# Half a block of padding ahead of PE's first turning, and batch 0's third turning in another order

## The chip, the cores and the metric

One core of one Trainium2 chip runs the kernel. The metric is the device time of one execution in microseconds (us). A single profiled execution gives the trace; the engines in it are PE (TensorE: matmuls, with PEld for its weight loads), DVE (VectorE), ACT (ScalarE), POOL (GpSimd) and SP (SyncE, here the queue that issues most DMAs).

## What is computed

Chunked attention over 4 batches, 8 heads, 768 positions, head size 64, followed by a mixer with a rank-32 product over the positions and a two-layer network over 512 channels. Everything is float32.

```
for c in range(nc):                       # chunks of 32, context 16 left, 8 right, 8 memory slots
    k_full = np.concatenate([mem_k, k_ctx], axis=2)
    v_full = np.concatenate([mem_v, v_ctx], axis=2)
    scores = scale * np.matmul(q_c, k_full.transpose(0, 1, 3, 2))
    a = np.exp(scores - max); a = a / (a.sum + 1e-09)
    out[:, :, c_start:c_end] = np.matmul(a, v_full)
x = out.transpose(0, 2, 1, 3).reshape(B, S, H * D)
u = x + (x^T @ U @ V)^T                   # U: 768 x 32, V: 32 x 768
result = u + np.maximum(u @ w_ch1, 0.0) @ w_ch2    # 512 -> 2048 -> 512
```

## The kernel before

Operands of the large products are split into a high and a low part (`uh`/`ul`, `w1h`/`w1l`, `w` as a pair, `hh`/`hl`), and three products of parts replace one. The weights U, V, w_ch1 and w_ch2 arrive as 64-bit words and are decoded on chip by a chain of steps (class `Words`, lines 235 to 281): `begin` on ACT, `shift`, `power`, `mantissa` and `join` on DVE (the join of some on POOL), then a cast to the high part on ACT and a subtraction for the low part (`lower`, line 420).

Batch 0 is a head that runs alone, written out by hand in `attention(0, xs)` (lines 840 to 980). Its 768 positions are taken in three parts, T = 0, 1, 2 ("turnings" of keys, queries and probabilities). For each T: `s_turn(T)` makes the scores (line 735), `s_weights` takes the maximum and the exponential into `pt`, `t_part(T, s)` turns the probabilities on PE (line 789) and copies them to `pT` on ACT (line 792), `av_part(T)` multiplies them with V's rows (64 fp32 matmuls, line 809, 128 records in the trace), `s_sums(T)` gives the row sums and their reciprocals (lines 766 to 771), and av_part then writes two tiles of x on DVE (four instructions, line 821). `collect(t)` (line 833) adds x(t) times the spread U to the rank product; `turn_x` (line 1184) turns x for the first block of the mixer; `spread_v` (line 300) copies V's three decoded column groups from 32-row groups to 96 rows with a matmul each (line 304), cast on ACT (line 309) and subtracted on DVE (line 310).

The words of a unit n of `stream()` are w1 of f=0, w2 of f=0, w1 of f=1, and so on; `advance(n)` moves that generator n steps, so its decoding steps stand in the engines' queues where `advance` is called. `take(n)` issues the next n loads of `LOADS`; `a0` is w1 of f=0, `b0` is w2 of f=0, `w1` and `w2` are w1 and w2 of f=1 and f=2. A load can be held back by a one-element copy on POOL into its target (`behind`, line 371): the load then waits for that copy, and the copy for the tile that it reads.

After the last collect, the rank product is cast to `g` in two halves (lines 1132, 1133), `join_uT` adds V times g to the turned x in PSUM (line 1193), the sums go to `uh` (line 1197) and `ul` (line 1198), and block 0 of the mixer begins: `w1_step(f)` (line 1534) and `w2_step(f)` (lines 1585, 1595) for f = 0, 1, 2, ... From here on PE follows a fixed order of units in which the attention of the next batches is mixed.

The order of all instructions on PE is the order of the code; on ACT and POOL it is so through the head, on DVE up to a later unit. PE is kept from falling idle by filler matmuls: `keep_clock(START, 512)` puts START wide ones of zeros ahead of the first turning (line 146), and `pad(ps, FILL)` puts FILL tiny ones (32x8, line 158) into PE's wait for g. A fp32 matmul becomes two weight loads and two matmuls in the program. PSUM tiles come from `bank()`: the names `ps_a`, `ps_h` and `acc` are pools of banks, and `asked` or `wide` tell which pool the next tile comes from.

Of the kernel before, what the change touches and what calls it, by code (L numbers as in the profile page):

```python
# [24 lines left out]
PACED = {ET.DVE}  # L25
HEAD = {ET.Activation, ET.Pool}
FIRST = 3000
START = 12
FILL = 17
PROBS = [5, 0, 9]  # L30
LOADS = 'mv t1 t2 uv v0 v1 a0 v2 b0 w1 w2'
WLO = 4
# [27 lines left out]
def chunk_attn_then_mixer_kernel(  # L60
# [13 lines left out]
    nc = tc.nc  # L74
# [42 lines left out]
    def w1_home(f, shape, dtype, name):  # L117
        return (w1q if f >= LASTW else w1r if f in (2 * NPL - 2, 2 * NPL - 1) else w1p).tile(shape, dtype, name=name, tag=f"w1_{f}")
# [24 lines left out]
    def att_ps():  # L143
        ps = bank()
        for width in warm:
            nc.tensor.matmul(out=ps[:, 0:width], lhsT=busy[:, 0:P], rhs=busy[:, 0:width], start=True, stop=True)
        warm.clear()
        return ps

    def keep_clock(n, width):  # L150

        warm.extend([width] * n)
# [146 lines left out]

    def spread_v(val):  # L300
        for g in range(VG):
            ps = att_ps()
            rows = slice(32 * g, 32 * g + 32)
            nc.tensor.matmul(
                out=ps[0:96, 0:VQ], lhsT=rep[rows].rearrange("p a b -> p (a b)"),
                rhs=val[rows, 0:VQ], start=True, stop=True,
            )
            c = slice(VQ * g, VQ * g + VQ)
            nc.scalar.copy(out=v3[:, c], in_=ps[0:96, 0:VQ])
            nc.vector.tensor_tensor(  # L310
                out=v3[32:64, c], in0=ps[32:64, 0:VQ], in1=v3[32:64, c].bitcast(F32), op=ALU.subtract,
            )

    def fetch_memk():
# [34 lines left out]
    def load_w1(f):  # L349
        a = []  # L350
        for h in range(2):
            if h == 0:
                raw = w1_home(f, [P, 256, 2], I32, "rw1")
            else:
                raw = slot([P, 256, 2], I32, "raw")
            nc.sync.dma_start(
                out=raw.rearrange("p (c n) two -> p c (n two)", c=2),
                in_=w1v[:, 2 * h:2 * h + 2, 2 * f * P:2 * (f + 1) * P],
            )
            a.append(raw)  # L360
        staged[f] = (a, [])

    behind = []

    def load_w2(f):
        c = staged[f][1]
        rows = w2[f * P:(f + 1) * P, :]
        if f < LASTF:
            raw = const.tile([P, CH, 2], I32, name="rw2", tag=f"w2_{f}")
            while behind:  # L370
                nc.gpsimd.tensor_copy(out=raw.bitcast(F32)[0:1, 0, 0:1], in_=behind.pop())
            nc.sync.dma_start(out=raw.rearrange("p n two -> p (n two)"), in_=rows)
            c.append(raw)
        else:
            for h in range(2):
                raw = slot([P, 256, 2], I32, "raw")
                nc.sync.dma_start(out=raw.rearrange("p n two -> p (n two)"), in_=rows[:, 512 * h:512 * h + 512])
                c.append(raw)
# [48 lines left out]
    def stream():  # L427

        work = [[(f, n)] for f in range(NSOLO) for n in range(2)] + [[(f, 0), (f, 1)] for f in range(NSOLO, NF)]

        def ready(n):
            return n < len(work) and work[n][0][0] in staged and not (front[0] and len(work[n]) > 1)

        def begun(n):
            words = Words([raw for f, which in work[n] for raw in staged[f][which]], decoder(n), turn=n)
            words.begin()
            return words

        while not ready(0):
            yield  # L440
        ahead, before = begun(0), []
        yield
        for n, parts in enumerate(work):
            if ahead is None and before:
                for part in before:
                    lower(*part)
                before = []
                yield
            while ahead is None and not ready(n):
                yield  # L450
            if n + 1 == len(work):
                for part in before:
                    lower(*part)
                before = []
                yield
            words, ahead = ahead or begun(n), None
            words.shift()
            if before:
                yield
                for part in before:  # L460
                    lower(*part)
            if len(parts) > 1 and n + 2 < len(work) and ready(n + 1):
                ahead = begun(n + 1)
            yield
            words.power()
            yield
            words.mantissa()
            yield
            if ahead is None and n + 2 < len(work) and ready(n + 1) and not held[0]:
                ahead = begun(n + 1)  # L470
            val = words.join()
            before = [(f, which, val[:, 512 * m:512 * m + 512]) for m, (f, which) in enumerate(parts)]
            before = [part + upper(*part) for part in before]
            yield
        for part in before:
            lower(*part)
        yield
# [67 lines left out]
    def attention(b, xs):  # L545
# [40 lines left out]
        def regroup(raws, groups, name, T):  # L586
            for h in range(2):
                if b >= DIRECT:
                    groups[T, h] = raws.pop((T, h))
                    continue  # L590
                if front[0]:
                    f = 5 + 4 * (T % 2) + 2 * (name == "qn") + h
                    groups[T, h] = w1_home(f, [P, 2, 4, D], F32, name)
                else:
                    groups[T, h] = slot([P, 2, 4, D], F32, name)
                (nc.gpsimd if b == 1 or front[0] and T == 2 else nc.vector).tensor_copy(
                    out=groups[T, h].rearrange("n r h d -> n h r d"),
                    in_=raws.pop((T, h)).rearrange("n h (r d) -> n h r d", r=2),
                )
# [142 lines left out]
        def s_weights(T, banks, psv, sides=range(2)):  # L742
            for s in sides:
                if T == 0:
                    nc.vector.memset(psv[s][0:CK, 0, :, :, NM:NM + LEFT], NEG)
                if T == NP - 1:
                    nc.vector.memset(psv[s][P - CK:P, 1, :, :, NW - 8:NW], NEG)
                if front[0]:
                    both = const.tile([P, 2, 512], F32, name="pt", tag=f"w2_{PROBS[T] + s}")
                    pt, pT[T, s] = both[:, 0], both[:, 1].rearrange("c (j n) -> c j n", j=4)  # L750
                else:
                    pt = slot([P, 512], F32, "pt")
                pts[T, s] = pt
                ptv = pt.rearrange("n (a w) -> n a w", w=NW)
                mx = sm.tile([P, 8], F32, name="mx", bufs=3)
                sc = banks[s].rearrange("n (a w) -> n a w", w=NW)
                nc.vector.tensor_reduce(out=mx, in_=sc, axis=AX.X, op=ALU.max)
                nc.vector.tensor_tensor(
                    out=ptv, in0=sc, in1=mx[:, :, None].broadcast_to([P, 8, NW]), op=ALU.subtract,
                )  # L760
                nc.scalar.activation(out=pt, in_=pt, func=AF.Exp, scale=scale)
# [82 lines left out]
        if b == 0:  # L844
# [33 lines left out]
            spread_mv(vbs[0])  # L878
            take(2)
            keep_clock(START, 512)  # L880
            regroup(kraw, kn, "kn", 0)
            for h in two:
                k_part(0, h)
# [47 lines left out]
                t_part(0, s)  # L931
            v_words.begin()
            s_weights(2, *sc)
            v_words.shift()
            v_words.low()
            val = v_words.join()
            av_part(0)
            s_sums(1)
            yield
            for s in two:  # L940
                t_part(1, s)
            for t in two:
                collect(t)
            av_part(1)
            for t in two:
                collect(2 + t)
            s_sums(2)
            asked.extend(["h", "h", "o0", "a", "a"])
            spread_v(val)
            wide[0] = None  # L950
            advance(1)
            for s in two:
                t_part(2, s)
            behind.append(pT[2, 0][0:1, 0, 0:1])
            take(len(loading))
            early = turn_x(range(NCK))
            next(early)
            next(early)
            yield
            advance(4)  # L960
            av_part(2)
            early = next(early)
            yield
            advance(3)
            for t in range(4, NT):
                collect(t)
            turned.extend(turn_x1(c) for c in range(3))
# [162 lines left out]
        for c in range(0, CH, width):  # L1130
# [3 lines left out]
                out=g3[64:96, cs], in0=gr[64:96, cs], in1=g3[64:96, cs].bitcast(F32), op=ALU.subtract,  # L1134
            )
        if b == 0:
            join_uT(early, g3)
            advance(1)
            for c in range(3):
                join_uT1(turned[c], c, g3)  # L1140
            held[0] = False
            rest.extend((c, g3) for c in range(3, NCK))
            ranks.append(g3)
# [611 lines left out]
```

## Time and profile before

| | us |
|---|---|
| runs (three): median, lowest, highest | 642.21, 641.68, 646.93 |
| the profiled execution | 642.83 |
| its span | 641.0 |
| PE busy | 616.5 (96%) |
| DVE, ACT, POOL busy | 379.8, 252.6, 140.5 |

The span is the time from the first to the last instruction that the profile counts; 1.8 us of the execution lie around it. Busy time is summed over the whole span. [...] In a timeline row the first number is the start, the second the time to the end of the group, and in brackets stands how long the engine was idle before it and what ended that. "issue" is time in which the engine waited for nothing that the profile shows.

### The profile page before, as it was taken

The page shows a single profiled execution, that of the slowest core. Times are in us where ns is not written, and L with a number is a line of the kernel's source. Part 1 is how long each engine was busy: PE and PEld are TensorE (multiplying, and loading weights), DVE is VectorE, ACT ScalarE, POOL GpSimd, SP SyncE. Part 2 cuts the span into 40 slices and gives each one's busy share as a digit, 9 for nine tenths or more (in the row PEclk, how much of TensorE's full clock was granted, in tenths as well). Part 3 has the DMA queues.
Part 4 walks back from the last instruction along what each step waited for, and adds up shares of the span by engine and source line. Part 5 has one row for each costly group of instructions (what it writes and reads, how often), then busy time and mean ns, then how long its engine had stood idle before and what let it go on. Part 6 is the DMA issues. An engine that isn't in the chain of part 4 may idle for free.

```text
span 641.0 us, 15102 instructions
## 1 busy us (share of the span) xinstructions
PE 616.5 (96%) x6002; PEld 533.2 (83%) x6002; DVE 379.8 (59%) x725; ACT 252.6 (39%) x635; POOL 140.5 (22%) x295
## 2 busy tenths in 40 slices
PE   7789999999899999999999999999999999999997
PEld 5548899988787888788888798999877899999886
DVE  6868788898694747844665735554466822222323
ACT  5526444348332545422255622321257622121221
POOL 5201000033263553321743100211335200000000
PEclk9889999999999999899999999999999999999999
DMA  8869577758788699476589759766422065565201
GB/s 237 166 209 363 175 240 247 221 181 173 172 192 230 175 317 282 137 201 160 164 243 215 151 177 307 201 182 187 124 82 77 0 199 164 149 181 153 93 0 49
DMA packets 168705, 115.02 MB, mean 179 GB/s; under 512 B 100956, under 2 KB 139484, under 8 KB 168636
## 3 DMA queue, kind: packets, MB, share of 16 engines
q1 hardware_dynamic: 168012, 113.92, 63.0%
q8 instruction: 47, 0.77, 0.5%
q10 hardware_dynamic: 624, 0.15, 0.1%
q14 instruction: 22, 0.18, 0.1%
HBM read 90.83 MB, written 28.97 MB: 187 GB/s over the span
## 4 chain that ended last, share of the span: by engine, by line
PE 57%; DVE 5%; ACT 3%; DMA 3%; POOL 2%; issue 2%; SPq 1%; ACTq 0%; POOLq 0%; DVEq 0%
PE ps_h L1354 24%; PE acc L1585 16%; PE acc L1595 8%; DMA blocks<-spread 2%; PE ps_a L809 2%; PE ps_h L1534 2%; ACT uc L183 1%; PE acc L1579 1%; PE ps_a L735 1%; POOL pt L183 1%; PE ps_a L839 1%; POOL vb L514 1%; DVE x L1550 1%; DMA w1l<-w1s 1%; DVE rs L766 1%
## 5 line engine op out<-in xcount | busy, mean ns | idle before, releaser
L1585 PE MATMUL acc<-w,hh 128*128 128x512 f32 x612 | 158.0, 393 | 1.6 <-ACT hh L1368 1.3
L1585 PEld LDWEIGHTS acc<-w,hh 128*128 128x128 f32 x612 | 113.2, 188 | 23.4 <-ACT hh L1368 2.8
L1595 PE MATMUL acc<-w,hl 128*128 128x512 f32 x306 | 86.9, 392 | 0.0
L1595 PEld LDWEIGHTS acc<-w,hl 128*128 128x128 f32 x306 | 56.9, 188 | 11.9
L1354 PE MATMUL ps_h<-t12h,w1l 128*128 128x384 f32 x192 | 55.5, 343 | 0.8 <-ACT c L1380 0.7
L1354 PE MATMUL ps_h<-bh,w1l 128*128 128x384 f32 x192 | 53.4, 342 | 0.0
L183 POOL COPY pt<-y 32x128 f32<-32x128 f32 x96 | 30.2, 315 | 97.9 <-DVE y L180 93.8
L1354 PE MATMUL ps_h<-t34h,w1l 128*128 128x384 f32 x152 | 45.9, 343 | 0.2 <-DMA w1l<-w1s 0.2
L183 POOL COPY uc<-y 32x128 f32<-32x128 f32 x96 | 32.7, 340 | 56.2 <-DVE y L180 52.4
L1534 PE MATMUL ps_h<-uh,w1h 128*128 128x384 f32 x124 | 42.0, 347 | 1.9 <-ACT w1h L413 1.9
L1369 DVE SCALAR_TENSOR_TENSOR hl<-ps_h,hh 128x384 fp32r<-128x384 f32 x29 | 16.1, 555 | 43.0 <-ACT hh L1368 42.9
L1534 PE MATMUL ps_h<-ul,w1h 128*128 128x384 f32 x124 | 40.7, 336 | 0.0
L1376 DVE TENSOR_TENSOR c<-ps_h,c 128x384 f32<-128x384 f32 x19 | 10.5, 554 | 49.6 <-PE ps_h L1354 49.6
L1369 DVE SCALAR_TENSOR_TENSOR hl<-hst,hh 128x384 fp32r<-128x384 f32 x36 | 20.7, 576 | 29.9 <-PE acc L1595 21.3
L1354 PEld LDWEIGHTS ps_h<-t12h,w1l 128*128 128x128 f32 x192 | 35.2, 188 | 3.7 <-ACT c L1380 1.0
L1354 PEld LDWEIGHTS ps_h<-bh,w1l 128*128 128x128 f32 x192 | 35.6, 190 | 0.9 <-issue 0.2
L1354 PE MATMUL ps_h<-b,w1l 128*128 128x384 f32 x174 | 35.5, 339 | 0.1
L1368 ACT ACTIVATE hh<-ps_h 128x384 fp32r<-128x384 f32 x29 | 14.2, 491 | 53.4 <-PE ps_h L1354 53.4
L1376 DVE TENSOR_TENSOR hst<-ps_h,hst 128x384 f32<-128x384 f32 x36 | 19.9, 553 | 23.8 <-ACT hst L1380 16.8
L1368 ACT ACTIVATE hh<-hst 128x384 fp32r<-128x384 f32 x36 | 18.8, 524 | 36.3 <-PE acc L1585 29.9
L1380 ACT COPY c<-ps_h 128x384 f32<-128x384 f32 x19 | 9.1, 479 | 59.0 <-PE ps_h L1354 59.0
L1354 PE MATMUL ps_h<-t12l,w1l 128*128 128x384 f32 x96 | 32.3, 337 | 0.0
(261 smaller groups left out, 1274.0 us busy)
## 6 DMA issues: line engine op xcount, KB each, us to landing
w1l<-w1s SPq DMA_DIRECT2D x155, 256.0 KB
rw<-in_moe_w_ch_dram SPq DMA_DIRECT2D x14, 512.0 KB
out_dram<-x SPq DMA_DIRECT2D x24, 256.0 KB
blocks<-spread SPq DMA_DIRECT2D x24, 256.0 KB
vb<-in_v_dram SPq DMA_DIRECT2D x56, 98.0 KB
raw<-in_moe_w_ch_dram SPq DMA_DIRECT2D x20, 256.0 KB
rw<-in_moe_w_ch_dram SPq DMA_DIRECT2D x16, 256.0 KB
w1s<-sums SPq DMA_DIRECT2D x16, 256.0 KB
```

Of the source, the lines that this page charges most:

```text
L183: (nc.scalar.copy if both and (5 * to + at) % 8 < 3 else nc.gpsimd.tensor_copy)(out=dst[CK * to:CK * to + CK, :, CK * at:CK * at + CK], in ...
L514: nc.gpsimd.tensor_tensor(out=out, in0=in0, in1=in1, op=op)
L735: nc.tensor.matmul(out=psv[s][(slice(CK * i, CK * i + CK), t) + ((p // 2, p % 2) if b >= DIRECT else (p % 2, p // 2))], lhsT=qt[p // 2][ro ...
L809: nc.tensor.matmul(out=psv[g][CK * i:CK * i + CK, t, j], lhsT=pt[s][rows, 2 * t + k_, CK * i:CK * i + CK], rhs=vt[rows, NI * t + i, D * j: ...
L1354: nc.tensor.matmul(out=ps[:, :TOK], lhsT=w_, rhs=u, start=(start and m == 0), stop=(m == 5), skip_group_check=True,)
L1368: nc.scalar.activation(out=hh, in_=c, func=AF.Relu)
L1369: nc.vector.scalar_tensor_tensor(out=hl, in0=c, scalar=0.0, in1=hh.bitcast(F32), op0=ALU.max, op1=ALU.subtract,)
L1376: nc.vector.tensor_tensor(out=out, in0=ps[:, :TOK], in1=in1, op=ALU.add)
L1380: nc.scalar.copy(out=out, in_=ps[:, :TOK])
L1534: nc.tensor.matmul(out=ph[:, :TOK], lhsT=w[:, c, :], rhs=u[c], start=(m == 0), stop=(m + 1 == len(parts)),)
L1585: nc.tensor.matmul(out=acc[tt], lhsT=h[:, sl], rhs=w, start=(begins and m == 0), stop=False,)
L1595: nc.tensor.matmul(out=acc[tt], lhsT=hl[:, sl], rhs=w2h[f], start=False, stop=ends is not None)
```

## The change

At the start, 6 wide filler matmuls in place of 12, then 35 tiny ones into the PSUM tile of the first turning. At PE's wait for g, 32 tiny ones in place of 17. In the head, the steps of V's decoding are issued behind x(0) and the sums of T=1; t_part(2) comes ahead of the spread of V, and the collects of x(1) behind it; spread_v uses halves of PSUM tiles of one pool; the decodings of f=0 are advanced at other places; and the loads of f=1 and f=2 are issued behind g, held by a copy from it.

```
-START = 12
-FILL = 17
+START = 6
+SHIFT = 35
+FILL = 32
...
         warm.clear()
+        if shift:
+            pad(ps, shift.pop())
         return ps
...
     def spread_v(val):
         for g in range(VG):
-            ps = att_ps()
+            if g % 2 == 0:
+                ps = att_ps()
+            half = ps[:, VQ * (g % 2):VQ * (g % 2) + VQ]
             rows = slice(32 * g, 32 * g + 32)
             nc.tensor.matmul(
-                out=ps[0:96, 0:VQ], lhsT=rep[rows].rearrange("p a b -> p (a b)"),
-                rhs=val[rows, 0:VQ], start=True, stop=True,
+                out=half[0:96], lhsT=rep[rows].rearrange("p a b -> p (a b)"),
+                rhs=val[rows, 0:VQ], start=True, stop=True, skip_group_check=True,
             )
             c = slice(VQ * g, VQ * g + VQ)
-            nc.scalar.copy(out=v3[:, c], in_=ps[0:96, 0:VQ])
+            nc.scalar.copy(out=v3[:, c], in_=half[0:96])
             nc.vector.tensor_tensor(
-                out=v3[32:64, c], in0=ps[32:64, 0:VQ], in1=v3[32:64, c].bitcast(F32), op=ALU.subtract,
+                out=v3[32:64, c], in0=half[32:64], in1=v3[32:64, c].bitcast(F32), op=ALU.subtract,
             )
...
     def load_w1(f):
...
                 raw = w1_home(f, [P, 256, 2], I32, "rw1")
+                hold(raw)
...
+    def hold(raw):
+        while behind:
+            nc.gpsimd.tensor_copy(out=raw.bitcast(F32)[0:1, 0, 0:1], in_=behind.pop())
...
             raw = const.tile([P, CH, 2], I32, name="rw2", tag=f"w2_{f}")
-            while behind:
-                nc.gpsimd.tensor_copy(out=raw.bitcast(F32)[0:1, 0, 0:1], in_=behind.pop())
+            hold(raw)
...
-            if ahead is None and n + 2 < len(work) and ready(n + 1) and not held[0]:
+            if ahead is None and n + 2 < len(work) and ready(n + 1) and (n == 0 or not held[0]):
                 ahead = begun(n + 1)
...
             keep_clock(START, 512)
+            shift.append(SHIFT)
             regroup(kraw, kn, "kn", 0)
...
             s_weights(2, *sc)
+            av_part(0)
+            s_sums(1)
             v_words.shift()
             v_words.low()
             val = v_words.join()
-            av_part(0)
-            s_sums(1)
             yield
...
             av_part(1)
-            for t in two:
-                collect(2 + t)
-            s_sums(2)
-            asked.extend(["h", "h", "o0", "a", "a"])
-            spread_v(val)
             wide[0] = None
-            advance(1)
             for s in two:
                 t_part(2, s)
             behind.append(pT[2, 0][0:1, 0, 0:1])
-            take(len(loading))
+            take(1)
+            s_sums(2)
+            spread_v(val)
+            for t in two:
+                collect(2 + t)
             early = turn_x(range(NCK))
             next(early)
             next(early)
+            advance(4)
             yield
-            advance(4)
             av_part(2)
             early = next(early)
+            advance(2)
             yield
-            advance(3)
             for t in range(4, NT):
                 collect(t)
...
         if b == 0:
+            behind.append(g3[0:1, 0:1].bitcast(F32))
+            take(len(loading))
+            advance(2)
             join_uT(early, g3)
```

How the instructions stand now is shown at three places. The line numbers are those of the kernel that the row belongs to; in brackets stands the semaphore that an instruction waits for, which is named by the engine that raises it.

PE between av(1) and the turning of x, before: two collects (`acc<-x,uarea`), three spread products (`dec,rep`), eight turnings of the probabilities, and the turning of x.

```order
L833 MATMUL acc_312<-x,uarea 96x512 [waits DVE_49] x2
L304 MATMUL ps_h<-dec,rep 96x256 [waits PE_49] x2
L304 MATMUL acc_819<-dec,rep 96x256
L789 MATMUL ps_a<-ident,pt 128x128 x8
L1184 MATMUL ps_h<-ident,x 128x128 [waits DVE_49] x2
```

The same place after the change:

```order
L800 MATMUL ps_a<-ident,pt 128x128 [waits PE_49]
L800 MATMUL ps_a<-ident,pt 128x128 x3
L800 MATMUL ps_a<-ident,pt 128x128 [waits PE_49]
L800 MATMUL ps_a<-ident,pt 128x128 x3
L311 MATMUL ps_a<-dec,rep 96x256 [waits DVE_49,PE_49]
L311 MATMUL ps_a<-dec,rep 96x256 [waits DVE_49]
L311 MATMUL ps_a<-dec,rep 96x256 [waits PE_49]
L844 MATMUL acc_341<-x,uarea 96x512 x2
L1197 MATMUL ps_h<-ident,x 128x128 x2
```

The collects have moved behind the turnings and the spread products, and the second spread product has a wait for DVE, in front of the collects.

DVE from the last x of T=1 to the first `ul`, before (`v` is the subtraction of spread_v, `dec` a decoding step of f=0):

```order
L766 TENSOR_REDUCE rs<-pt 128x2x2x2 [waits Activation_49] x2
L770 TENSOR_SCALAR rs<-rs 128x16 [waits DVE_49]
L771 RECIPROCAL rs<-rs 128x16 [waits DVE_49]
L310 TENSOR_TENSOR v_111<-ps_h,v_111 32x256 [waits Activation_49] x2
...
L420 TENSOR_TENSOR w1l<-dec,w1h_870 128x512 [waits Activation_49]
L259 TENSOR_SCALAR dec<-dec 128x512 [waits Activation_49]
L267 TENSOR_SCALAR dec<-dec 128x512 [waits DVE_49]
L1133 TENSOR_TENSOR g_985<-acc_312,g_985 32x256 [waits Activation_49] x2
L1198 TENSOR_TENSOR ul<-ps_h,uh 128x384 [waits Activation_49,Pool_49]
```

The same after the change:

```order
L777 TENSOR_REDUCE rs<-pt 128x2x2x2 [waits Activation_49] x2
L781 TENSOR_SCALAR rs<-rs 128x16 [waits DVE_49]
L782 RECIPROCAL rs<-rs 128x16 [waits DVE_49]
L317 TENSOR_TENSOR v_111<-ps_a,v_111 32x256 [waits Activation_49] x3
...
L264 TENSOR_SCALAR dec<-dec 128x512 [waits Activation_49]
L1143 TENSOR_TENSOR g_1014<-acc_341,g_1014 32x256 [waits Activation_49] x2
L431 TENSOR_TENSOR w1l<-dec,w1h_964 128x512 [waits DVE_49]
L272 TENSOR_SCALAR dec<-dec 128x512 [waits DVE_49]
L1211 TENSOR_TENSOR ul<-ps_h,uh 128x384 [waits Activation_49,Pool_49]
```

The three `v` subtractions stand behind the sums of T=2 as before, and the w1l subtraction and one power step have moved behind the two halves of g.

PE's first rows after the change (from the last wide filler to the turning of the memory keys); before, twelve wide ones stood directly ahead of the turning of `kn`:

```order
L147 LDWEIGHTS busy
L147 MATMUL ps_a<-busy 128x512
L163 MATMUL ps_a<-ident 32x8 x35
L658 MATMUL ps_a<-ident,kn 128x128 x4
L658 MATMUL ps_h<-ident,kn 128x128 x4
L335 MATMUL ps_a<-ident,mk 128x128
```

All rows of PE behind the 35 tiny matmuls have moved back by 128 instructions, and those behind the second filler by another 60.

## Rows read from the trace of the kernel before

**Rows 1.** The page: busy time, granted clock in 40 slices, instruction queue (packets, MB, share).
```profile
PE 616.5 (96%) x6002; PEld 533.2 (83%) x6002; DVE 379.8 (59%) x725; ACT 252.6 (39%) x635; POOL 140.5 (22%) x295
...
PEclk9889999999999999899999999999999999999999
...
q8 instruction: 47, 0.77, 0.5%
```

**Rows 2.** Busy time by stretches: PE, PEld, DVE, ACT, POOL; PEclk, DMA share, GB/s.
```profile
28.40:31.80 3.40, 3.40 (x75) 1.49 (x78) 1.58 (x4) 0.00 (x0) 0.00 (x0) 0.50 0.87 189
...
42.00:45.40 3.40, 3.34 (x30) 1.82 (x30) 2.62 (x7) 0.67 (x1) 0.00 (x0) 0.51 1.01 355
57.70:70.00 12.30, 12.30 (x62) 11.21 (x63) 10.50 (x18) 6.74 (x15) 0.00 (x0) 1.00 0.77 262
```

**Rows 3.** Timeline of PE from 27 to 58 us: start, duration, instruction, idle before.
```profile
27.76 3.14 PE L833 MATMUL acc<-x,uarea 128*96 128x512 f32 x4 [2.09 <-DVE x L821]
...
33.47 1.96 PE L833 MATMUL acc<-x,uarea 128*96 128x512 f32 x4 [0.83 <-DVE x L821]
...
36.93 0.66 PE L1184 MATMUL ps_h<-ident,x 128*128 128x128 f32 x2
...
38.41 1.33 PE L809 MATMUL ps_a<-vbe,pt 64*32 64x64 f32 x105
42.06 0.65 PE L809 MATMUL ps_a<-vbe,pt 64*32 64x64 f32 x23 [2.33 <-issue]
...
43.56 2.88 PE L833 MATMUL acc<-x,uarea 128*96 128x512 f32 x4
...
47.35 0.48 PE L158 MATMUL ps_a<-ident 32*32 32x8 f32 x34
...
57.68 0.96 PE L1534 MATMUL ps_h<-uh,w1h 128*128 128x384 f32 x4 [0.74 <-ACT w1h L413]
```

**Rows 4.** DMA queues from 39.3 to 40.8 us: packets, MB, share.
```profile
q8 instruction: 1, 0.02, 5.5%
```

**Rows 5.** Timeline of PE: the other places where it idled for "issue".
```profile
15.72 0.21 PE L735 MATMUL ps_a<-kall,qt 64*32 64x64 f32 x1 [0.38 <-issue]
...
23.33 0.24 PE L809 MATMUL ps_a<-vb,pt 64*32 64x64 f32 x1 [0.56 <-issue]
...
195.33 0.29 PE L809 MATMUL ps_a<-vb,pT 64*32 64x64 f32 x9 [0.38 <-issue]
```

**Rows 6.** Timeline of PE: the first filler and the turning behind it.
```profile
1.47 4.24 PE L146 MATMUL ps_a<-busy 128*128 128x512 bf16 x12 [1.47 <-DVE kall L214]
...
6.86 0.66 PE L647 MATMUL ps_h<-ident,kn 128*128 128x128 f32 x4 [0.71 <-DVE kn L596]
```

**Rows 7.** Timeline of DVE from 25 to 49 us.
```profile
25.52 0.28 DVE L259 TENSOR_SCALAR dec<-dec 96x256 int32<-96x256 int32 x1
...
26.96 0.41 DVE L821 TENSOR_TENSOR x<-ps_h,rs 128x256 f32<-128x256 f32 x1
...
33.99 1.27 DVE L766 TENSOR_REDUCE rs<-pt 128x8 f32<-128x512 f32 x2
...
35.51 0.25 DVE L771 RECIPROCAL rs<-rs 128x16 f32<-128x16 f32 x1
...
42.75 1.42 DVE L821 TENSOR_TENSOR x<-ps_a,rs 128x256 f32<-128x256 f32 x4 [2.69 <-PE ps_a L809]
44.08 0.68 DVE L420 TENSOR_TENSOR w1l<-dec,w1h 128x512 fp32r<-128x512 f32 x1
...
45.14 0.43 DVE L267 TENSOR_SCALAR dec<-dec 128x512 int32<-128x512 int32 x1
...
47.74 0.42 DVE L1133 TENSOR_TENSOR g<-acc,g 32x256 fp32r<-32x256 f32 x1 [0.43 <-ACT g L1132]
48.82 1.02 DVE L1198 TENSOR_TENSOR ul<-ps_h,uh 128x384 fp32r<-128x384 f32 x2 [0.66 <-ACT uh L1197]
```

**Rows 8.** Timeline of SP's queue and of ACT: a load of w2 of f=0, and who waited for it.
```profile
38.61 0.36 SPq L372 DMA_DIRECT2D rw<-in_moe_w_ch_dram  x1
...
43.04 0.67 ACT L252 ACTIVATE dec<-rw 128x512 f32<-128x512 f32 x1 [2.27 <-DMA rw<-in_moe_w_ch_dram]
```

More of the change, by code (lines that the diff above doesn't have):

```diff
@@ L147, in att_ps @@
         warm.clear()
+        if shift:
+            pad(ps, shift.pop())
         return ps
+    shift = []
     def keep_clock(n, width):
```

## Prediction

> **What bounds the kernel now.** I read the page first: TensorE is busy for 96% of the span at a granted clock near full [rows 1]. Then the same stretch by stretch. From 57.7 us on PE leaves no gap (12.30 of 12.30 us) [rows 2], so whatever the change gains or loses before that point is gained or lost at the end, microsecond for microsecond, unless it also makes gaps later. The question is therefore one number: when does the f=1 unit of block 0 start, now 57.68 us [rows 3]? Last come the timelines of PE, VectorE (DVE) and the loads between 25 and 58 us. [...] (a) PE waits 2.09 us for the x tiles of the first turning, until 27.76. (b) In av(2) PE stands still for 2.33 us after 105 of 128 matmuls, and no semaphore ends the gap: the row says "issue" [rows 3]. [...]
>
> **What gap (b) is.** In its stretch one packet of the instruction queue moves, 0.02 MB [rows 4]; the page has 47 of them with 0.77 MB, 16 KB each [rows 1]. Counted through PE's order (a fp32 matmul is two loads and two matmuls), the three places in the head where PE idles for "issue", up to 15.72, 23.33 and 42.06 us [rows 3, 5], have numbers that leave the same remainder, 194, when divided by 256, and so has the fourth at 195.33. I read this as: PE's program comes in pieces of 256 instructions, and PE stands when it has run through one before the next is there. That the gap has another cause stands among the rivals. [...]
>
> **The change part by part.**
>
> Start. Six warm matmuls go (4.24 us for 12, so -2.1 us), 35 pads come (0.48 us for 17, so +1.0 us) [rows 3, 6]. The turning of kn behind them waits for DVE anyway (0.71 us before 6.86) [rows 6]: worth 0. If this thinner start cost clock, the head's later rows hide it up to that wait.
>
> Shift. Ahead of the first turning PE gets 140 pad instructions and loses 12, so +128: every piece boundary moves by half a piece. The old one sat 210 instructions into av(2) (105 matmuls and their loads); the new one sits 82 into it, and the piece before it now starts in av(1). Between these two PE has the transposes of t_part(2), the spreads of V, two collects and the turning of x, over 6 us by [rows 3], where gap (b)'s piece was entered near 35.4. So I take the 2.33 us as gone, and keep the whole 2.33 us as the bound on the other side.
>
> Third turning, DVE side. The four decoding steps of V's words run from 25.52 to 26.96, ahead of x(0) [rows 7]; they now stand behind x(0) and the sums of T=1. So x(0) starts 1.44 us earlier, the first collects at 26.32, and wait (a) is 0.65 us. Then I expect no half clock here: 1.96 us in place of 3.14, end at 28.3. av(1) follows; when its V rows landed no row tells, since PE was busy with the collects until 30.9. Bounds: 28.3 and 30.9; I take 29.5, between them, 1.4 us earlier than before. The decoding ends near 30.1 (x(0) to 26.9, then the sums and 1.44 us), before av(1) is through: hidden.
>
> Third turning, PE side. The three spread products now use two halves of one bank and one of a second, and come ahead of collects 2 and 3. In the order the second product waits for a DVE event, which it did not do before: the first `v` subtraction, out of the same bank. On DVE that subtraction stands behind x(1) and the sums of T=2 (1.76 us from 33.99 to 35.76, where x(1) ended at 33.99) [rows 7]. With av(1) 1.4 us earlier the sums end at 34.4 and the subtraction (0.4, as those of g) at 34.8; two more products (under 0.5 us each, from half a collect: 1.96/4) put collects 2, 3 at about 35.5, where they stood at 33.47 [rows 3]. Behind the waiting product stand collects 2 and 3, the turning of x, av(2): all of PE. With av(1) at 28.3 or 30.9 the collects start at 34.3 or 36.8. The wait is about 2.4 us, as long as gaps (a) and (b), so I expect the half clock here instead: collects 3.1 us, to 38.6 (1.96 us if not). [...] The order shows that wait, and no row of before has one like it.
>
> av(2). Turning x before it takes 38.41 - 36.93 = 1.48 us [rows 3]: av(2) from 40.1, and without the gap 1.33 x 128/105 = 1.6 us, so x(2) from 41.75 against 42.75 [rows 7]: 1.0 us gained. Collects 4 and 5 start 0.8 us behind it and, no gap before them, run at full clock, 1.96 against 2.88 us: 1.9 us gained at their end. If the clock stays low through them, 1.0.
>
> Filler. Fifteen more pads at 0.48/17 us are 0.42 us. They fill PE's wait for the rank product g; g now comes earlier, so I charge them in full: 1.5 us gained when the join starts.
>
> Decodings. w1l's subtraction and the power step (0.68 + 0.43 us) stood before g, while DVE waited, and now stand behind it; before, DVE idled 0.66 us between g (48.16) and `ul` (48.82) [rows 7], so 0.45 us of the 1.11 is late: f=1 gains 1.05 us.
>
> Loads. One copy is added on GpSimd: the loads of w1(1), w2(1) and w(2) now wait on SyncE's queue for the first half of g. The nearest row: the w2(0) load, issued at 38.61, ended ScalarE's wait at 43.04, 4.4 us later [rows 8]. With the collects through at 44.5 half of g is there near 45 us, the copy takes about half a us, so w1(1) lands near 50 us. What hides it is DVE's own work on `ul`, which began at 48.82 and takes over 2 us [rows 7]. Covered, with little to spare; without that cover f=1 is late by what is missing.
>
> Later boundaries. One stall of 0.38 us (195.33) [rows 5] should go. But the new boundaries open pieces at places where PE runs through 256 instructions in some 3 to 4 us (score products, av), about five after 57.7 us. Each may cost from 0 (as nearly all of the 40 now do) to 0.56 us, the longer of the small stalls [rows 5]. I take 0.4 in all, by the row that nearly all boundaries show: no loss. Net 0.
>
> Sum against the profiled execution (642.83 us, span 641.0): -1.05 us, so 641.8. The runs shown have a median 0.6 us under that execution: 641.2 us.
>
> **Rivals.**
>
> R1, faster: DVE's wait is short. V's rows for av(1) are there at 28.3, so collects 2, 3 start at 34.3 (1.2 us better), PE's gap is then too short for the half clock (1.2 us better), and part of the pads is hidden. Gain 1.05 + 2.4 + 0.2 = 3.6 us: 638.6 by the median. For it: both half-clocked rows follow gaps of over 2 us [rows 2, 3]. Against: DVE still has 3.5 us to do between av(1) and the subtraction.
>
> R2, slower: the new boundaries cut the fast stretches. Five pieces of score products or av stall PE for 0.56 us each, +2.8, less the 0.38: +2.4; and w1(1), held behind g, comes as f=1 would gain, so f=1 keeps 57.68. 642.21 + 2.4 = 644.6 us. It decides once PE enters such a piece with the next one less than the passing time away. For it: 15.72, 23.33 and 195.33 are just such stalls. Against: they are three of about 40.
>
> R3, the change doesn't do what it says: a stall comes back in av(2), whose boundary is only moved, or the gap has another cause. Then 2.33 us and the half clock of collects 4, 5 (0.92 us) return: -1.05 + 3.25 = +2.2, so 644.4 us. For it: a piece still ends inside av(2). Against: four stalls at one remainder. [...]
>
> R4, the wait eats everything: V late (30.9) and half clock at 35 to 39 us. Collects 2 and 3 at 36.8: +1.3 on the sum, 642.5 us.
>
> **How the numbers follow.** Forecast 0.42 (its own range 640 to 642.4); R1 0.25, R4 0.10, R2 0.15, R3 0.08. The range of 637.2 to 644.8 takes in the losses of R2 and R3 and the gain of R1 with 1.4 us more, about the half-clocked loss of one stretch. About 1% (6.4 us) is what a measurement of this kernel can tell from no change. Faster by that needs twice R1's gain: 0.05. Slower by that needs R2 and R3 together: 0.03. Within: 0.92.
>
> **What would show it.** Right: no "issue" gap in av(2); the first PE wait for x under 1 us; a PE wait of 2 to 3 us for the first `v` subtraction at the second spread product; half clock near 35 to 38 us and none near 42; f=1 starting near 56.6 us. Wrong: half clock nowhere and f=1 before 55 us (R1); issue stalls after 57.7 us of over 1 us in all, or w1(1) ending ScalarE's wait (R2); an "issue" gap over 1 us in av(2) (R3).

## The result and the profile after

The changed kernel takes 650.24 us (median of 13 runs, 645.72 to 653.01), the kernel before 643.19 us (13 runs beside it): slower, ratio 1.0104 with a 95% interval of 1.0078 to 1.013. Forecast was 641.2, with a range of 637.2 to 644.8. The profiled execution takes 648.51 us, 5.7 more than that of before. Two executions far outside the rest, 753.63 us of the kernel before and 1521.02 us of one kernel below (`FILL = 32`), are in no median and no ratio of this text.

The page of the changed kernel answers to [rows 1]: PE has 94 matmuls more, the instruction queue one packet more, and the clock is lower at the start.

```profile
span 646.7 us, 15291 instructions
...
PE 617.9 (96%) x6096; PEld 534.7 (83%) x6096; DVE 379.6 (59%) x725; ACT 252.8 (39%) x635; POOL 141.9 (22%) x296
...
PEclk7889999999999999999999999999999999999999
...
q8 instruction: 48, 0.79, 0.5%
```

PE's waits up to 58 us in the changed kernel (what waits and for what: us in total, times, the longest):

```profile
PE ps_h L746 <- issue: 4.5, 2, 2.9
PE ps_a L311 <- DVE v L317: 2.5, 1, 2.5
PE ps_a L746 <- issue: 2.0, 1, 2.0
...
PE ps_a L820 <- issue: 1.1, 1, 1.1
...
PE acc L844 <- DVE x L832: 0.3, 1, 0.3
```

The reader is to see that the wait for x has shrunk to 0.3 us (2.9 us before), that the foretold wait for `v` has come, and that "issue" has risen from 3.3 to 7.6 us, at other lines. L746 is the score product (L735 before). The timeline of PE says where:

```profile
15.97 0.21 PE L746 MATMUL ps_h<-kall,qt 64*32 64x64 f32 x1 [1.58 <-issue]
...
22.28 0.24 PE L746 MATMUL ps_h<-kall,qt 64*32 64x64 f32 x1 [2.94 <-issue]
...
27.30 0.24 PE L746 MATMUL ps_a<-kall,qt 64*32 64x64 f32 x1 [1.97 <-issue]
...
32.62 0.21 PE L820 MATMUL ps_a<-vb,pt 64*32 64x64 f32 x1 [1.06 <-issue]
...
41.60 1.16 PE L311 MATMUL ps_a<-dec,rep 32*96 32x256 f32 x4 [2.47 <-DVE v L317]
42.69 3.12 PE L844 MATMUL acc<-x,uarea 128*96 128x512 f32 x4
...
46.62 1.48 PE L820 MATMUL ps_a<-vbe,pt 64*32 64x64 f32 x128
...
48.95 1.96 PE L844 MATMUL acc<-x,uarea 128*96 128x512 f32 x4 [0.27 <-DVE x L832]
...
51.82 0.71 PE L163 MATMUL ps_a<-ident 32*32 32x8 f32 x64
...
62.63 0.98 PE L1547 MATMUL ps_h<-uh,w1h 128*128 128x384 f32 x4 [0.81 <-ACT w1h L424]
```

Four stalls stand in the score products and in av(0), and av(2) runs its 128 matmuls without one. f=1 starts at 62.63 instead of 57.68 us [rows 3]: of the 5.7 us, 4.95 are there before f=1, 0.7 come later. Counted through PE's order, all four stalls again stand at a number that leaves 194 (or 195) when divided by 256. In the longest one a packet of the instruction queue moves, here from 19.4 to 22.3 us:

```profile
q8 instruction: 1, 0.02, 2.0%
```

The packet times in the traces of all 14 kernels say more than this row. Each trace has one such packet per 256 instructions of PE (47 packets of 16 KB for 12004 matmul and load records before, 48 for 12192 here). Matched in order, PE enters none of 655 pieces sooner than 1.17 us after its packet's end. The 46 "issue" gaps of over 1 us all stand at this remainder, and each ends 1.17 to 1.71 us after its packet (1.48 in the one above). So PE stood there for its next piece.

The granted clock by stretches (PEclk, as a share of full speed), as in [rows 2]:

```profile
7.50:10.90 3.40, 2.49 (x13) 2.33 (x12) 2.19 (x9) 1.14 (x5) 0.74 (x2) 0.50 1.08 311
10.90:14.30 3.40, 3.40 (x128) 2.92 (x127) 1.97 (x5) 2.00 (x10) 2.33 (x3) 0.50 1.14 316
28.00:31.40 3.40, 3.12 (x91) 2.50 (x90) 2.87 (x6) 2.33 (x5) 0.36 (x1) 0.50 0.80 180
41.70:45.10 3.40, 3.40 (x7) 1.25 (x8) 1.67 (x5) 1.85 (x5) 0.00 (x0) 0.50 0.03 13
```

Four such rows in the head (the first two cover 7.5 to 14.3 us) stand where before had two: up to and through the first score product, behind the stall at 27.30, and behind the wait for `v`. The clock granted in them is 0.50.

### The profile page after: what moved, and what is told of

Read it like the earlier page. It is cut to its first block, busy times and chain, and to the rows that moved or that the text cites. A ratio compares the mean times of both kernels' runs of the same rounds, so it can differ in the third digit from the quotient of the medians.

```text
span 646.7 us, 15291 instructions
## 1 busy us (share of the span) xinstructions
PE 617.9 (96%) x6096; PEld 534.7 (83%) x6096; DVE 379.6 (59%) x725; ACT 252.8 (39%) x635; POOL 141.9 (22%) x296
## 4 chain that ended last, share of the span: by engine, by line
PE 57%; DVE 5%; DMA 3%; ACT 3%; POOL 2%; issue 1%; SPq 1%; ACTq 0%; POOLq 0%; DVEq 0%
PE ps_h L1367 24%; PE acc L1598 16%; PE acc L1608 8%; PE ps_a L820 2%; DMA blocks<-spread 2%; PE ps_h L1547 2%; DMA w1l<-w1s 2%; ACT uc L188 1%; PE acc L1592 1%; PE ps_a L746 1%; POOL pt L188 1%; PE ps_a L850 1%; DVE x L1563 1%; DVE rs L777 1%; DVE mx L768 1%
## 5 line engine op out<-in xcount | busy, mean ns | idle before, releaser
L1367 PE MATMUL ps_h<-t12h,w1l 128*128 128x384 f32 x192 | 55.8, 344 | 1.2 <-ACT c L1393 0.6
```

The costliest lines, as they stand in the source:

```text
L1367: nc.tensor.matmul(out=ps[:, :TOK], lhsT=w_, rhs=u, start=(start and m == 0), stop=(m == 5), skip_group_check=True,)
```

## The experiments

Theory P: PE's time depends on where the ends of its 256-instruction pieces fall; an end in a stretch that PE runs through fast is a stall. Rival W: the wait of the second spread product for DVE is the loss. Rival C: the thinner start costs clock. Two more came up on the way: A, the losses behind f=1 come from the new order; D, moving the ends does nothing of its own. Twelve kernels were run, each beside the kernel before. Differences in us are the ratio's, of some 643.5 us. A time inside a kernel, such as the start of f=1 or a stall, is of one execution, the profiled one; it can lie some us from the median run.

**One part alone, and parts undone.** The first takes the start of the change alone into the kernel before:

```
-START = 12
+START = 6
+SHIFT = 35
...
+        if shift:
+            pad(ps, shift.pop())
```

> The kernel before with the start of the changed one alone (6 wide fillers, 35 tiny ones; nothing of the third turning). Theory P (the 256-instruction pieces now end inside the head's score products): the four stalls of the changed kernel's head, 1.58, 2.94, 1.97 and 1.06 us, are here too, 7.6 us against 3.3 us before, and the half clock at 8.4 to 15 us; no stall in av(2). Before + 4.7 us (3.5 to 6). Rival W (the wait of the second spread product for DVE is the loss): before, within 1 us. Rival C (the thinner start costs clock, nothing else matters): before + 2 us.

Measured: 656.13 us, ratio 1.0183 (1.0142 to 1.0224), +11.8 us by the ratio. Worse than the whole change, and not as P said: its head has the four stalls (2.11, 1.05, 1.15, 1.32 us) and no stall in av(2), but f=1 is only 1.3 us late. The rest, some 9 us, comes behind f=1; these are its two longest waits:

```profile
270.70 0.37 PE L814 MATMUL ps_a<-vb,pT 64*32 64x64 f32 x9 [2.01 <-issue]
...
404.60 0.41 PE L1360 MATMUL ps_h<-t12h,w1l 128*128 128x384 f32 x1 [2.25 <-DMA w1l<-w1s]
```

The issue stall at 270.70 has the same remainder, and the clock stands at half for two stretches around it (0.51 from 268.9 us, 0.50 from 272.3 to 275.7). The second wait is for a load and no piece end; P does not explain it. One of about 2 us stands near there in two other kernels with the shift too, so not all of the 9 us is P's.

The second, against the changed kernel, leaves the start as before and keeps the third turning:

```
-START = 6
-SHIFT = 35
+START = 12
 FILL = 32
...
-            shift.append(SHIFT)
```

> The changed kernel without its shift: 12 wide fillers at the start as before, no tiny ones there; the third turning in the new order. Theory P: stalls as before (0.38, 0.56, and one of up to 2.3 in av(2)), and the DVE wait of about 2.5 us at the second spread product; before + 0.5 us (-1 to +2). Rival W: the loss stays, before + 4 to 7. Rival C: before, within 1 us, but with the stalls of the score products still there.

Measured: 651.95 us, ratio 1.0128 (1.0082 to 1.0174), +8.2 us, outside what P said. But its f=1 starts at 55.9 us, 1.8 earlier than before. The loss is all later, with issue stalls of 2.56 us at 188.65 and 1.20 us at 305.25, at remainder 194; they are about half of the 7.7 us lost there in this execution. So the order of the third turning was not the loss; the 15 more tiny matmuls at g, which move all later pieces by 60 instructions, were suspected.

The third is the changed kernel with 256 instead of 128 instructions added at the start (`SHIFT = 67`).

> The changed kernel with 67 tiny matmuls in place of 35, so that everything behind them stands a whole piece (256 instructions) later than before, and the pieces end where they ended before. Theory P: the stalls of the score products go although more is added; the thin start stays. Before + 1.5 us (-0.5 to +3.5). Rival C: the half clock at 8.4 to 15 us stays and with it the loss, as the changed kernel. Rival W: as the changed kernel, before + 5 to 7.

Measured: 653.4 us, ratio 1.0145 (1.0104 to 1.0187), +9.3 us. P's part on the head held: two of the stalls in the score products are gone and a third is 0.36 us, f=1 is at 58.7 instead of 62.6 us, though more was added; a new one of 2.00 us stands in t_part(2). Its sum did not, for the same reason as above: the later pieces end as in the run before, and the same two stalls are there, 3.11 us at 192.05 and 1.19 at 308.46.

The fourth gives the spread of the changed kernel its three banks back:

```
-            if g % 2 == 0:
-                ps = att_ps()
-            half = ps[:, VQ * (g % 2):VQ * (g % 2) + VQ]
+            ps = att_ps()
+            half = ps[:, 0:VQ]
...
+            asked.extend(["a", "a", "h", "h", "o0"])
             for s in two:
                 t_part(2, s)
```

> The changed kernel with the three spread products in three banks, as before: the second one waits for no DVE event. Theory P: the 2.5 us wait goes, collects 2 and 3 start when x(1) is there (about 39.5 instead of 42.7 us) at full clock; f=1 some 3 us earlier; the stalls of the score products stay. Before + 4 us (2.5 to 5.5). Rival W: all of the loss goes, before within 1 us. Rival C: as the changed kernel.

Measured: 646.29 us, ratio 1.0032 (1.0004 to 1.006), +2.1 us, 4.6 less than the whole change. No wait for `v` is left; the collects start at 40.38 us (42.69 in the changed kernel) and at full clock:

```profile
40.38 1.96 PE L843 MATMUL acc<-x,uarea 128*96 128x512 f32 x4
```

f=1 comes 3.0 us earlier. So W is part of the loss, somewhat more than P allowed, and not all of it: the stalls of the score products and of av(0) stay (2.47, 1.39, 1.42 and 2.08 us). The profiled execution was the slowest of the twelve (650.35 us): behind f=1 it loses 5.6 us against the kernel before, with a wait of 2.08 us for a load at 402.00 and one of 1.52 for ACT at 244.14, and only 0.9 us of stalls at piece ends.

**Where pieces end, with nothing else changed.** Only the number of tiny matmuls at g (`FILL = 32` in the kernel before):

> The kernel before with 32 tiny matmuls in place of 17 at the wait for g, and nothing else: up to there it is the kernel before, all later pieces end 60 instructions earlier in the program, as in the run with the reorder alone. Theory P (loss where a piece of 256 instructions is run through in under some 4 us): issue stalls near 190 and 303 us of about 2.6 and 1.2 us, as there, and a late DVE near 155; f=1 at 57.7 +- 0.5 and the end later by 4 to 6 us: before + 5. Rival A (the later losses come from the order of the third turning and its later loads): before, within 1 us.

Measured: 651.98 us, ratio 1.0129 (1.0097 to 1.0161), +8.3 us for fifteen tiny matmuls whose own time is 0.23 us (0.71 us for 64 records against 0.48 for 34). f=1 is 1.1 us late (the stall in av(2) was 3.42 us in this execution), the rest comes later, for the most part from the waits that P named: 2.56 us at 191.77 and

```profile
306.51 0.30 PE L735 MATMUL ps_a<-kall,qt 64*32 64x64 f32 x8 [1.25 <-issue]
```

and a late DVE at 156.98 (1.47 us). In the 2.5 us just ahead of the stall at 191.77, PE ran 126 matmuls and 126 loads, nearly a piece, without a gap:

```profile
186.70:189.20 2.50, 2.50 (x126) 1.68 (x126) 2.50 (x6) 0.78 (x2) 0.56 (x1) 1.00 1.00 349
```

Rival A falls, and the run explains the 8.2 us of the reorder alone: that kernel has the same 32.

The same with less work (`FILL = 7`):

> The kernel before with 7 tiny matmuls in place of 17 at g: 40 instructions less, and by the times that PE takes from piece end to piece end in the trace of before the worst place for all later ends: pieces of 1.4 to 2.6 us near 164, 196, 250, 280, 412 and 438 us. Theory P: six issue stalls of 1.5 to 3 us there, before + 9 us (6 to 14), though work is taken out. Rival A: before, within 1 us.

Measured: 647.78 us, ratio 1.008 (1.005 to 1.011), +5.1 us. Work was taken out and it got slower, as P said, but by half of what P said: one of the six places stalled in the profiled execution, the others did not.

```profile
196.39 0.34 PE L1534 MATMUL ps_h<-uh,w1l 128*128 128x384 f32 x1 [3.03 <-issue]
```

So a piece that is run through fast may stall PE, not must. Counted over the traces of all 14 kernels, pieces that PE ran through in under 4 us ended in an "issue" gap of over 1 us 32 times in 96, those of 4 to 6 us 11 times in 99, slower ones 3 times in 460. PE ran through the fast pieces that ended in such a gap and through those that did not in the same time (median 3.3 us). What differs is the packet of the next piece: it began 2.3 us after PE had entered the fast piece in the first case, 0.2 in the second (medians). What sets its start is not shown.

**The thin start** (6 wide and 3 tiny, the same number of instructions):

> The kernel before with 6 wide fillers and 3 tiny ones at the start: 12 instructions out, 12 in, so that every piece ends where it ended. Theory C (thin start costs clock): half clock between 8 and 15 us and before + 2. Theory P: before, within 1 us; the half clock alone, in a stretch that waits for loads, costs under 1 us.

Measured: 645.01 us, ratio 1.0008 (0.999 to 1.0026): no difference that can be measured, so C falls as the cause of the loss. Its trace has no half clock before 27 us, so the run does not price the one that the changed kernel has from 7.5 to 14.3 us. Five other kernels with the same six wide fillers and 35 tiny ones have none there either. The same trace shows how far a stall's size moves at ends that did not move: 1.80, 1.12, 1.22 and 2.59 us in the head, 6.7 in all, against 3.3 in the kernel before.

**The two fillers together, and one taken back.** The kernel before with both fillers of the change, and the changed kernel with `FILL = 17`:

> The kernel before with both fillers of the changed one (6 wide, 35 tiny at the start, 32 at g) and the old third turning. Theory P: the head as in the run with the shift alone (f=1 at 59 +- 1), the later pieces as in the changed kernel, with under 1 us of loss: before + 2.5 (1 to 5). So the two fillers, which cost 8 and 12 us each alone, cost little together, and the rest of the changed kernel's 7 us is its spread in halves. Rival D: they add up, before + 15 or more.

> The changed kernel with 17 tiny matmuls at g, as before, in place of 32. Theory P: the head is that of the changed kernel (f=1 near 62.5), but the later pieces now end where they ended in the run with the shift alone, which lost 9 us behind f=1: before + 12 (9 to 15), an issue stall near 270 us of some 2 us. Rival D (the filler has no effect beyond its own time): as the changed kernel, before + 7.

Measured: 649.78 us, ratio 1.0096 (1.0063 to 1.013), +6.2 us, for the first; 661.37 us, ratio 1.027 (1.0238 to 1.0301), +17.4 us, for the second. They don't add up to the 20 us of each alone, but 6.2 is more than the 5 that P allowed; its profiled execution was the fastest of its eight runs (644.03 us) and has only three stalls in the head, so where the median loses is not seen. The second run is clear: taking away fifteen tiny matmuls of 0.23 us makes the changed kernel 10.7 us slower, since the later pieces then end where the shift alone puts them:

```profile
277.99 0.42 PE L820 MATMUL ps_a<-vb,pT 64*32 64x64 f32 x10 [1.82 <-issue]
```

and another of 2.65 us stands at 195.01. Rival D falls. It is the 32 that keep these stalls away in the changed kernel.

**The wait for `v`.** In the changed kernel, on DVE, the subtractions go ahead of the sums of T=2:

```
-            s_sums(2)
             spread_v(val)
+            s_sums(2)
```

> The changed kernel with the v subtractions ahead of the sums of T=2 on DVE, everything else the same. Theory W: the wait of the second spread product (2.47 us) falls by the 1.8 us of the sums, the half clock in the collects behind it may go too; f=1 some 2 us earlier: before + 4.5 (3 to 6.5). Rival: the sums are then late for x(2) or the half clock stays: as the changed kernel, before + 7.

Measured: 647.46 us, ratio 1.0067 (1.0036 to 1.0098), +4.3 us, 2.4 less than the changed kernel. The wait falls as W said, and the collects behind it run at full clock:

```profile
38.96 0.67 PE L311 MATMUL ps_a<-dec,rep 32*96 32x256 f32 x4 [0.91 <-DVE v L317]
39.56 1.96 PE L844 MATMUL acc<-x,uarea 128*96 128x512 f32 x4
```

**The new order without its costs.** Three banks, both fillers as before, so that the pieces end where they ended:

> The third turning in the new order with the loads behind g, but three banks for the spread, 12 wide fillers, no tiny ones at the start and 17 at g: every piece ends where it ended before, within one instruction. Theory P: the head gains (f=1 at 54.5 to 56.5), no later stall but the 0.38 us one; before - 2 (-3.5 to -0.5). Rival A: the order itself costs; before + 3 or more.

Measured: 643.01 us, ratio 0.9987 (0.9965 to 1.0008): no difference that can be measured, where P had 2 us. f=1 starts 1.9 us earlier (55.8), less than it could: a piece now ends in the turning t_part(2), behind a faster stretch, and one still in av(2):

```profile
34.28 0.33 PE L798 MATMUL ps_a<-ident,pt 128*128 128x128 f32 x1 [2.41 <-issue]
...
40.83 0.29 PE L818 MATMUL ps_a<-vbe,pt 64*32 64x64 f32 x9 [1.42 <-issue]
```

So the last run moves the ends by 176 instructions (`SHIFT = 47`, `FILL = 17`, three banks):

> The new order with three banks, 6 wide and 47 tiny fillers at the start (+176 instructions) and 17 at g. Theory P: no issue stall near 34 and 41 us (2.4 and 1.4 us in the run with the same pieces as before), pieces end inside the score products near 15, 19 and 22 us instead, 0 to 1.6 us each; later ends at about the second best place: before - 1.5 (-4 to +1.5). Rival D: as the run with the new order and the old pieces, before - 0.6 within 0.6.

Measured: 641.1 us, ratio 0.9959 (0.9942 to 0.9977), -2.6 us: faster than both kernels, if little. No stall stands in t_part(2) or av(2), and f=1 starts at 53.2, 4.5 us earlier than before. But the span is only 0.7 us shorter: matmul by matmul, PE is 5.2 us ahead of the kernel before at 190 us, 2.5 at 254 and 0.8 at 445. The largest steps lie between 190 and 254 us. There DVE waits for the blocks of the next batch, ACT for DVE, and the copy of `hst` stands behind that on ACT, with PE waiting for it:

```profile
226.35 0.71 DVE L675 STREAM_TRANSPOSE kall<-blocks 128x512 f32<-128x512 f32 x1 [2.12 <-DMA blocks<-spread]
```
```profile
227.09 0.38 ACT L676 COPY kall<-kall 128x224 f32<-128x224 f32 x1 [1.76 <-DVE kall L675]
227.38 0.47 ACT L1393 COPY hst<-ps_h 128x384 f32<-128x384 f32 x1
```
```profile
227.91 0.44 PE L1367 MATMUL ps_h<-bh,w1h 128*128 128x384 f32 x1 [1.14 <-ACT hst L1393]
```

The kernel before has the same chain, with the smaller wait on PE:

```profile
230.60 0.71 DVE L665 STREAM_TRANSPOSE kall<-blocks 128x512 f32<-128x512 f32 x1 [2.04 <-DMA blocks<-spread]
```
```profile
232.15 0.44 PE L1354 MATMUL ps_h<-bh,w1h 128*128 128x384 f32 x1 [0.38 <-ACT hst L1380]
```

The transfer ends DVE's wait 4.25 us earlier than there, PE is ready 5.0 us earlier, and so PE's wait grows by 0.76 us. A like wait of 0.91 us follows at 253.7 (0.05 before); why the transfers gain less than PE is not shown.

## Why the prediction was wrong

The account by the ratios: both fillers in the old order +6.2; with the new order and three banks +2.1, so that order gains about 4 there; with the spread in halves +6.7, so the halves cost 4.6. By the intervals each of these differences holds to within some 2 to 3 us. With the old piece ends the gain of the new order is not clear of noise (0.8 us), with other ends (`SHIFT = 47`) it is 2.6 us.

*What bounds the kernel*: half right. PE is the bound, but the row without a gap covers 57.7 to 70 us alone, and "one number", the start of f=1, does not give the end: f=1 came 1.8 us earlier in the second run and the time was 8.2 us longer, and 4.5 us earlier in the last with 2.6 us gained. The condition "unless it also makes gaps later" was the rule here.

*What gap (b) is*: right. All issue stalls of PE of over 0.3 us in these runs but one kind (0.3 us at the first turning of a later batch, the same in each kernel) stand at the end of a piece, and in each of the 46 long ones PE goes on 1.17 to 1.71 us after the end of its packet. The longest took 3.42 us (in av(2), with `FILL = 32`). R3 falls.

*Shift*: here lies the error. The step took the 2.33 us in av(2) as gone, which held (x128 in 1.48 us, no gap), but priced no other end in the head. The ends that it moved into the three score products and av(0) cost 1.58 + 2.94 + 1.97 + 1.06 = 7.55 us, against 0.38 + 0.56 + 2.33 = 3.27 before. The sum left 0.38 and 0.56 standing; the other 6.6 us are what it lacked, and f=1, foretold at 56.6, came 6.0 us later than that. The first x starts at 33.33 instead of 26.96 us, 6.4 late, although 1.44 us of decoding had left the place ahead of it. These are single executions: the four kernels with the ends and the order of before in the head show 3.3 to 6.7 us of such stalls there (mean 4.6), the six with the shift 4.8 to 8.0 (mean 6.6). So the shift's price in the head is more like 2 us than 4 (an estimate from these means); that the two fillers together cost some 6 us rests on the runs, not on one trace.

*Later boundaries*: put at 0, right for the changed kernel's profiled execution by luck (0.7 us lost behind f=1) and wrong as a rule: 60 instructions there cost 8.3 us, 40 less cost 5.1. The three other kernels with the same later ends lost 0.5, 2.9 and 5.6 us behind f=1 in theirs, and for most of that no stall at a piece end stands in the trace. R2 had the mechanism; its 0.56 us per piece was a half to a fifth of what single stalls took (1.2 to 3.1 us), and it looked behind 57.7 us alone, where the same stretches stand in the head too. The rows gave the clue: of three stalls in the head two were small and one was 2.33 us, and the step took the small ones for the price and the large one for a place.

*Third turning*: right, nearly to the number. In the changed kernel the stalls hide the first wait for x, but in the run with the new order and the old piece ends x(0) starts at 25.60 us (25.52 foretold) and the first collects at 26.40 (26.32) behind a wait of 0.55 (0.65). In the changed kernel the wait for `v` is 2.47 us (2.4), the collects behind it run at half clock in 3.12 us (3.1), and collects 4 and 5 at full clock in 1.96. The half clock was expected behind gaps of over 2 us; it stood behind one of 1.97 too (0.50 from 28.0 us), and not behind the one of 2.94 that ended at 22.28 (1.00 up to 28.0). What was missed is that the wait is not needed for the rest of the order: with three banks it is gone and the rest stays.

*Start*: 0, held by the run with the thin start, as far as the time goes. *Filler*: charged at 0.42 us, it took 0.23 more (0.71 us for 64 records), and this is beside the point; it moves the later pieces. *Decodings and loads*: ACT's wait for the w1(1) load did not come; f=1 waited for the same cast as before, 0.81 us against 0.74.

Open stays what makes a packet start late, and so why a fast piece stalls one time and not the next; what the median runs of the kernel with both fillers lose; and the waits for loads and for ACT behind f=1. Whether the other transfers in the DMA queues have a part in it was not tried.

## What to carry to other kernels

Where PE runs hundreds of short instructions in a few microseconds, the place of each 256th was part of the schedule here: count it through the program, look at how long each piece takes, and treat a filler anywhere ahead as an edit to everything behind it. Judge a reordering with the piece ends held fixed, or its gain and the shift's loss are read as one. A second product into the other half of the same bank brought a wait for the reader of the first half (2.47 us): look where that reader stands in its engine's queue. A stall's size in one trace is one draw (3.3 and 6.7 us in the head at the same ends): price an end by several kernels or runs.

## What was not expected of the hardware

Fifteen tiny matmuls with 0.23 us of work of their own moved the time by +8.3 us in one kernel, and taking the same fifteen out of another moved it by +10.7. A stall at a piece end reached 3.42 us, and stretches at half clock stood at several of them (two in a row, 6.8 us at 0.51 and 0.50, around the one at 270.70 in the kernel with the shift alone).
